# Two steps of VectorE's exponential chain placed on GpSimd, with a placing rule for the chain's products

## The chip, the cores and the metric

One core of one Trainium2 chip. The time is device time of one execution in microseconds (us). A run has a state: "slow" if it lies over 1.5% above the fastest run of the same kernel. The mean granted clock of TensorE is given with a run: 1.0 is full speed.

## The reference

```python
x = A_x                                   # 1 x 2048 x 640, bf16
xn = layernorm(x)
q, k, v = split_heads(xn @ wqkv)          # 32 heads of 20
s = softmax(q @ k.T * 20 ** -0.5) @ v @ wo
g = silu(mlp_over_tokens(layernorm(xn)))  # gelu inside, 2048 -> 1536 -> 2048
out = x + s * g
```

The softmax needs 32 x 2048 x 2048 exponentials. The kernel cuts them into 2048 units, each one PSUM bank of scores: 128 keys x 512 queries.

## The kernel before

A list scheduler in Python builds a fixed order of instructions for each engine, from a table of costs. At run time each engine follows its order and waits only on semaphores. TensorE (PE) writes scores into PSUM banks. ScalarE (ACT) takes two banks at a time through its exponential. VectorE (DVE) takes single banks (two of them, 4 and 5, each with its own buffers) through a chain of six instructions that builds the bits of an approximate exponential:

```python
ch = [
    (lambda e: e.tensor_scalar(w3, lo, 0x7FFF, None, ALU.bitwise_and), bs, [sw], dv(N)),            # mask, from PSUM
    (lambda e: e.tensor_scalar(v_, w_, 1.0 / 256.0, -128.0, ALU.mult, ALU.add), [sw], [sv], dv(N, .26)),   # linear
    (lambda e: e.tensor_scalar(l_, w_, a3 / 65536.0, (b3 - 64.0 * a3) / 256.0, ALU.mult, ALU.add),
     [sw], [sl_], dv(N, .26)),                                                                      # linear
    (lambda e: e.tensor_tensor(l_, v_, l_, ALU.mult), [sv, sl_], [sl_], dv(N, .52)),                # product
    (lambda e: e.tensor_tensor(l_, l_, w_, ALU.mult), [sl_, sw], [sl_], dv(N, .52)),                # product
    (lambda e: e.scalar_tensor_tensor(o_, zr, -(self.OFFS - 16256.0), l_, ALU.add, ALU.add),
     bs + [sl_], [S_(f"dpt{s0 + i}") for i in range(n)], dv(N)),                                    # last, from PSUM
]
# ... cut: the scheduler, each time an engine is free, takes the candidate that is ready first ...
if eng == "dve":
    for chn in dchains:
        (fn, rd, wr, cost) = chn[0][0]
        c.append((90.0 - 0.1 * len(chn), pr.ready("dve", rd, wr), lambda chn=chn: emit_dchain(chn)))
```

How many units go to DVE is not fixed: the scheduler gives it a new one whenever a DVE bank is free in its own clock. The rest stays with ACT.

The softmax here doesn't subtract the row's maximum and nothing guards it: scores larger than these inputs give would overflow.

Of the kernel before, what the change touches and what calls it, by code (L numbers as in the profile page):

```python
# [7 lines left out]
ALU = mybir.AluOpType  # L8
# [274 lines left out]
class _Kern:  # L283
# [25 lines left out]
    DVE_TAIL_GUARD = 3  # L309
    LAST_GUARD = 10  # L310
    NTMP = 4
    WARM = True
    WARM_MIN = 180.0
    WARM_SLACK = 30.0
# [87 lines left out]
    def schedule(self):  # L402
        pr, t = self.prog, self.t
# [21 lines left out]
        def S_(name):  # L425
            s = sl.get(name)
            if s is None:
                s = sl[name] = _Slot(name)
            return s
# [12 lines left out]
        def dv(n, rate=1.04):  # L442
            return 75.0 + n * rate
# [51 lines left out]
        def small(fn):  # L495
            def f(e):
# [12 lines left out]
                name="id1", cost=300)  # L509
# [5 lines left out]
               cost=200)  # L515
# [8 lines left out]
               writes=[S_("pad")], name="pad", cost=150)  # L524
        pr.dve(lambda e: e.tensor_reduce(cst_sb[:, 1:2], onerow, mybir.AxisListType.X, ALU.add), reads=[S_("idf")],
               writes=[S_("row")], name="pad", cost=130)
        for col, a_, b_, src in ((3, -1.0, 1.0, 0), (4, -CQ0, CQ0, 0), (5, QC, 0.0, 1), (6, KC, 0.0, 1)):
            pr.dve(lambda e, col=col, a_=a_, b_=b_, src=src: e.tensor_scalar(
                cst_sb[:, col:col + 1], cst_sb[:, src:src + 1], a_, b_, ALU.mult, ALU.add),
                reads=[S_("pad"), S_("row")], writes=[S_("cq")], name="cq", cost=90)  # L530
# [535 lines left out]
        dexp = []  # L1066
# [79 lines left out]
        def can_exp():  # L1146
            if not pexp:
                return False
            n = len(pexp[0][0])
            s0 = ptr[0] if ptr[0] + n <= self.RP else 0  # L1150
            return not any(pt_busy[s0:s0 + n])

        dchains = []

        def start_dchain():

            us, banks, grp = dexp[0]
            n = len(us)
            if dptr[0] + n > self.DPT:
                dptr[0] = 0  # L1160
            s0 = dptr[0]
            dexp.pop(0)
            for i in range(n):
                dpt_busy[s0 + i] = True
            dptr[0] = (s0 + n) % self.DPT
            N = n * 512
            zr = ps_all[:, banks[0] * 512:banks[0] * 512 + N]
            lo = zr.bitcast(u16).rearrange("p (n two) -> p n two", two=2)[:, :, 0:1]
            k = self.DVE_GROUPS.index(grp)
            w_, v_, l_ = ew_sb[:, k, 0:N], ev_sb[:, k, 0:N], el_sb[:, k, 0:N]  # L1170
            sw, sv, sl_ = S_(f"ew{k}"), S_(f"ev{k}"), S_(f"el{k}")
            w3 = w_.rearrange("p (n one) -> p n one", one=1)
            o_ = dpt_sb[:, s0:s0 + n, :].rearrange("p a b -> p (a b)").bitcast(u16)
            bs = [bank_slot[b] for b in banks[:n]]
            a3, b3 = self.C3
            ch = [
                (lambda e: e.tensor_scalar(w3, lo, 0x7FFF, None, ALU.bitwise_and), bs, [sw], dv(N)),  # L1177
                (lambda e: e.tensor_scalar(v_, w_, 1.0 / 256.0, -128.0, ALU.mult, ALU.add), [sw], [sv], dv(N, .26)),  # L1178
                (lambda e: e.tensor_scalar(l_, w_, a3 / 65536.0, (b3 - 64.0 * a3) / 256.0, ALU.mult, ALU.add),  # L1179
                 [sw], [sl_], dv(N, .26)),  # L1180
                (lambda e: e.tensor_tensor(l_, v_, l_, ALU.mult), [sv, sl_], [sl_], dv(N, .52)),  # L1181
                (lambda e: e.tensor_tensor(l_, l_, w_, ALU.mult), [sl_, sw], [sl_], dv(N, .52)),  # L1182
                (lambda e: e.scalar_tensor_tensor(o_, zr, -(self.OFFS - 16256.0), l_, ALU.add, ALU.add),  # L1183
                 bs + [sl_], [S_(f"dpt{s0 + i}") for i in range(n)], dv(N)),
            ]
            dchains.append([(x, us, s0, grp) for x in ch])

        def emit_dchain(chn):
            (fn, rd, wr, cost), us, s0, grp = chn.pop(0)
            tk = pr.dve(fn, reads=rd, writes=wr, name=f"dexp{us[0]}", cost=cost)  # L1190
            if not chn:
                dchains.remove(chn)
                dgrp_state[grp] = "free"
                for i, u in enumerate(us):
                    avail.append((tk.fin, u, "d", s0 + i))
# [320 lines left out]
        def pe_cands(T):  # L1516
# [29 lines left out]
            if avail and acc_ok[0]:  # L1546
# [14 lines left out]
                if pick:  # L1561
                    r = max(x[0] for x in pick) + PV_MARGIN
                    pr_ = 1.0 if nav >= self.PV_HI else 30.0 if ramp[0] else (8.0 if pr.gate.warm or not self.WARM else 70.0)
                    c.append((pr_, max(r, pr.ready("pe", [], [sl_acc])), lambda pick=pick: emit_pv(pick)))
            if self.WARM:
                wb = warm_bank()
# [18 lines left out]
            for j in active:  # L1585
                s = j.steps[j.i]
                if s[0] == "pe":
                    c.append((j.prio if pr.gate.warm or not self.WARM else -2.0, pr.ready("pe", s[2], s[3]),
                              lambda j=j: do_step(j, "pe")))
# [60 lines left out]
        def do_step(j, eng):  # L1650
            s = j.steps[j.i]
            j.i += 1
            if s[0] == "ev":
                n = s[8]
                fn = ev_fn(s, eng)
                cost = ac(n) if eng == "act" else dv(n, 0.55 if s[7].startswith("xTe") else 1.04)
                getattr(pr, eng)(fn, reads=s[5], writes=s[6], name=s[7], cost=cost)
            elif s[0] == "pe":
                pe_full(s[1], s[2], s[3], s[4], s[5])
            else:  # L1660
                getattr(pr, s[0])(s[1], reads=s[2], writes=s[3], name=s[4], cost=s[5])
            settle(j)

        def eng_cands(eng, T):
            c = []
            for j in active:
                s = j.steps[j.i]
                if s[0] == eng:
                    c.append((j.prio, pr.ready(eng, s[2], s[3]), lambda j=j: do_step(j, eng)))
                elif s[0] == "ev" and (eng == "dve" or (eng == "act" and (ramp[0]))):  # L1670
                    pen = 0.0 if eng == "dve" else 0.0
                    c.append((j.prio - 30.0 + pen, pr.ready(eng, s[5], s[6]), lambda j=j: do_step(j, eng)))
            if eng == "act" and can_exp():
                us, banks, grp = pexp[0]
                c.append((30.0 if ramp[0] else 48.0, pr.ready("act", [bank_slot[b] for b in banks[:len(us)]], []), emit_exp))
            if eng == "dve":
                for chn in dchains:
                    (fn, rd, wr, cost) = chn[0][0]
                    c.append((90.0 - 0.1 * len(chn), pr.ready("dve", rd, wr), lambda chn=chn: emit_dchain(chn)))
                if dexp and not any(ch[0][3] == dexp[0][2] for ch in dchains):  # L1680
                    us, banks, grp = dexp[0]
                    n = len(us)
                    s0 = dptr[0] if dptr[0] + n <= self.DPT else 0
                    if not any(dpt_busy[s0:s0 + n]):
                        r = pr.ready("dve", [bank_slot[b] for b in banks[:n]], [])

                        def go():
                            start_dchain()
                            emit_dchain(dchains[-1])
                        c.append((90.0, r, go))  # L1690
            return c

        def warm_bank():
            if nxt[0] < 12:
                return AB
            if WB in busybanks or WB in bank_off:
                return None
            return WB
# [18 lines left out]
        while True:  # L1717
# [26 lines left out]
            for e in order:  # L1744
                cs = pe_cands(pr.T[e]) if e == "pe" else eng_cands(e, pr.T[e])
                cs_by[e] = cs

            bt = None
            for e in order:
                if not cs_by[e]:  # L1750
                    continue
                r = min(max(x[1], pr.T[e]) for x in cs_by[e])
# [4 lines left out]
            r, e = bt  # L1757
            if e == "dve" and nxt[0] >= NU:

                soon = [max(x[1], pr.T[e]) for x in cs_by[e] if x[0] <= 12.0]  # L1760
                if soon and min(soon) <= r + 130.0:
                    r = min(soon)
# [45 lines left out]
```

## Time and profile before

| | us |
|---|---|
| time, median of 2 runs | 869.83 (867.17 to 872.49) |
| span of the profiled run | 864.8, clock 1.0 |
| busy: PE, DVE, ACT, GpSimd | 798.6, 823.5, 845.3, 14.0 |

Lines of the profile are read in the prediction; "idle before" is how long the engine stood still just ahead of these instructions, and what ended it.

### The profile page before, as it was taken

To read this page: it belongs to the slowest core of one execution; us is meant where nothing else is said; L and a number is where in the kernel's file an instruction comes from. 1 tells how busy PE (TensorE), PEld (TensorE's weight loads), DVE (VectorE), ACT (ScalarE), POOL (GpSimd) and SP (SyncE) were. 2 spreads that over 40 slices of the span, in tenths; PEclk is the share of its full clock that TensorE was granted. 3 is DMA by queue.
4 is the path that set the end of the run, shared out by engine and by line. 5 is a ranking of instruction groups with operands and counts; after the bars stand their busy time and mean duration, and the time that the engine had idled before them with its cause. 6 is when DMAs were issued, how large, how long until landed. Compare 5 with 4: busy or idle time off the path is not lost.

```text
span 864.8 us, 16498 instructions
## 1 busy us (share of the span) xinstructions
PE 798.6 (92%) x5828; PEld 257.1 (30%) x5918; DVE 823.5 (95%) x2047; ACT 845.3 (98%) x925; POOL 14.0 (2%) x23
## 2 busy tenths in 40 slices
PE   8899999999999999999999999999899998998997
PEld 5422222222222223222322222222222222232233
DVE  8889999999999999999999999999999999999996
ACT  7899999999999999999999999999999999999996
POOL 3200000000000000000000000000000000000000
PEclk9999999999999999999999999999999999999999
DMA  8241010011010313020013022123312201032121
GB/s 236 48 113 30 8 35 10 16 36 31 11 55 15 77 34 89 10 55 10 16 25 78 23 51 52 25 52 71 67 30 46 47 11 11 3 102 69 41 44 35
DMA packets 123350, 39.32 MB, mean 45 GB/s; under 512 B 84312, under 2 KB 122152, under 8 KB 123272
## 3 DMA queue, kind: packets, MB, share of 16 engines
q1 hardware_dynamic: 123272, 38.27, 19.3%
q8 instruction: 50, 0.82, 0.4%
q14 instruction: 28, 0.23, 0.1%
HBM read 25.88 MB, written 9.83 MB: 41 GB/s over the span
## 4 chain that ended last, share of the span: by engine, by line
ACT 87%; PE 10%; DVE 2%; issue 1%; ACTq 0%
ACT pt_sb L1137 85%; PE ps_all L1109 3%; PE ps_all L1224 1%; ACT zt_sb L843 1%; PE ps_all L755 1%; PE ps_all L1702 1%; PE ps_all L879 1%; ACT zt_sb L838 1%; DVE ew_sb L1177 0%; PE ps_all L683 0%; PE ps_all L1710 0%; PE ps_all L722 0%; PE ps_all L703 0%; DVE dpt_sb L1183 0%; DVE el_sb L1181 0%
## 5 line engine op out<-in xcount | busy, mean ns | idle before, releaser
L1137 ACT ACTIVATE pt_sb<-ps_all 128x1024 bf16<-128x1024 f32 x888 | 819.8, 1144 | 3.8 <-PE ps_all L1109 3.0
L1109 PE MATMUL ps_all<-qk_sb 32*128 32x512 bf16 (+1 forms) x2112 | 367.5, 377 | 48.7 <-ACT pt_sb L1137 37.0
L1177 DVE TENSOR_SCALAR ew_sb<-ps_all 128x512 uint16<-128x512 uint16 x272 | 184.2, 685 | 20.7 <-PE ps_all L1109 19.6
L1109 PEld LDWEIGHTS ps_all<-qk_sb 32*128 32x128 bf16 x2112 | 97.3, 91 | 347.2 <-ACT pt_sb L1137 300.7
L1183 DVE SCALAR_TENSOR_TENSOR dpt_sb<-ps_all,el_sb 128x512 uint16<-128x512 f32 x272 | 182.1, 684 | 1.8
L1224 PE MATMUL ps_all<-pt_sb,v_sb 128*32 128x512 bf16 (+1 forms) x1833 | 162.7, 378 | 0.3 <-issue 0.3
L1181 DVE TENSOR_TENSOR el_sb<-ev_sb,el_sb 128x512 bf16<-128x512 bf16 x272 | 111.1, 418 | 1.1
L1182 DVE TENSOR_TENSOR el_sb<-el_sb,ew_sb 128x512 bf16<-128x512 bf16 x272 | 110.3, 418 | 0.9
L1224 PE MATMUL ps_all<-dpt_sb,v_sb 128*32 128x512 bf16 (+1 forms) x279 | 83.7, 379 | 0.0
L810 PE MATMUL ps_all<-regB,regA 128*128 128x128 bf16 (+1 forms) x371 | 75.6, 300 | 2.9 <-issue 1.1
L1178 DVE TENSOR_SCALAR ev_sb<-ew_sb 128x512 bf16<-128x512 uint16 x272 | 75.3, 285 | 2.3
L810 PE MATMUL ps_all<-regC,regA 128*128 128x128 bf16 (+1 forms) x370 | 74.2, 300 | 1.8 <-issue 1.0
L1179 DVE TENSOR_SCALAR el_sb<-ew_sb 128x512 bf16<-128x512 uint16 x272 | 75.1, 284 | 0.0
L722 PE MATMUL ps_all<-xnT_sb,wqk_sb 128*112 128x512 bf16 x200 | 68.2, 405 | 0.4 <-DVE zt_sb L816 0.4
L1224 PEld LDWEIGHTS ps_all<-pt_sb,v_sb 128*32 128x32 bf16 x1833 | 35.4, 94 | 55.5 <-issue 50.4
L1702 PE MATMUL ps_all<-wrm_sb 128*128 128x512 bf16 (+1 forms) x117 | 35.2, 391 | 3.9 <-DVE ps_all L513 2.2
L810 PEld LDWEIGHTS ps_all<-regB,regA 128*128 128x128 bf16 x384 | 25.8, 97 | 39.1 <-issue 23.8
L810 PEld LDWEIGHTS ps_all<-regC,regA 128*128 128x128 bf16 x384 | 25.0, 97 | 39.8 <-issue 28.5
L1710 PE MATMUL ps_all<-wrm_sb,v_sb 128*128 128x512 bf16 x97 | 34.0, 385 | 1.3 <-issue 0.7
L755 PE MATMUL ps_all<-wv_sb,xnT_sb 128*128 128x160 bf16 (+1 forms) x160 | 33.8, 302 | 0.4 <-DVE pk_sb L1030 0.3
L879 PE MATMUL ps_all<-wo_sb,xnT_sb 128*128 128x128 bf16 (+3 forms) x152 | 30.4, 298 | 0.7 <-issue 0.5
L722 PEld LDWEIGHTS ps_all<-xnT_sb,wqk_sb 128*112 128x112 bf16 x200 | 20.7, 127 | 30.6 <-issue 13.4
(89 smaller groups left out, 354.9 us busy)
## 6 DMA issues: line engine op xcount, KB each, us to landing
regA<-in_B_w_dram SPq DMA_DIRECT2D x6, 1024.0 KB
regA<-in_B_w_dram SPq DMA_DIRECT2D x8, 768.0 KB
qkT_scratch_dram<-pk_sb SPq DMA_DIRECT2D x40, 112.0 KB
qk_sb<-qkT_scratch_dram SPq DMA_DIRECT2D x56, 80.0 KB
regA<-in_A_x_dram SPq DMA_DIRECT2D x6, 640.0 KB
on_scratch_dram<-on_sb SPq DMA_DIRECT2D x124, 20.0 KB
out_dram<-regC SPq DMA_DIRECT2D x3, 640.0 KB
wqk_sb<-in_A_wqkv_dram SPq DMA_DIRECT2D x2, 680.0 KB
```

Of the source, the lines that this page charges most:

```text
L722: steps.append(("pe", lambda e, dc=dc: e.matmul(ps_all[0:112, bk * 512:(bk + 1) * 512], wqk_sb[:, dc * 1280 + c0:dc * 1280 + c0 + 112], xn ...
L810: steps.append(("pe", lambda e, k=k: e.matmul(ps(bk, n), wap[:, k, col0:col0 + 128], rows[:, k, c0:c0 + n], start=(k == 0), stop=(k == nk ...
L1109: pr.pe(lambda e, outp=outp, lhsT=lhsT, rhs=rhs, g=g: e.matmul(outp, lhsT, rhs, start=True, stop=True, tile_position=(32 * g, 0)), reads=q ...
L1137: tk = pr.act(lambda e: e.activation(outp, inp, AF.Exp, bias=-self.OFFS * math.log(2.0) / 128.0, scale=math.log(2.0) / 128.0), reads=[bank ...
L1177: (lambda e: e.tensor_scalar(w3, lo, 0x7FFF, None, ALU.bitwise_and), bs, [sw], dv(N)),
L1178: (lambda e: e.tensor_scalar(v_, w_, 1.0 / 256.0, -128.0, ALU.mult, ALU.add), [sw], [sv], dv(N, .26)),
L1179: (lambda e: e.tensor_scalar(l_, w_, a3 / 65536.0, (b3 - 64.0 * a3) / 256.0, ALU.mult, ALU.add), [sw], [sl_], dv(N, .26)),
L1181: (lambda e: e.tensor_tensor(l_, v_, l_, ALU.mult), [sv, sl_], [sl_], dv(N, .52)),
L1182: (lambda e: e.tensor_tensor(l_, l_, w_, ALU.mult), [sl_, sw], [sl_], dv(N, .52)),
L1183: (lambda e: e.scalar_tensor_tensor(o_, zr, -(self.OFFS - 16256.0), l_, ALU.add, ALU.add), bs + [sl_], [S_(f"dpt{s0 + i}") for i in range( ...
L1224: pr.pe(lambda e, outp=outp, lhsT=lhsT, rhs=rhs, k=k, g=g: e.matmul(outp, lhsT, rhs, start=(k == 0), stop=(k == NB - 1), tile_position=(0, ...
L1702: pe_full(lambda e: e.matmul(ps(wb, n), wrm_sb[:, 0:P], wrm_sb[:, P:P + n], start=True, stop=True), [S_("warm"), S_("warm1")], [bank_slot[ ...
```

## The change

Intent: DVE is nearly full, GpSimd is empty. Put the two linear steps on GpSimd. I expected the products to collide with GpSimd's steps; that was not shown by the trace before, and the trace after shows it (beside a step they take 491 and 653 ns on the mean, elsewhere 419 and 417). So let DVE take a product (flag `port` in the code) only when the GpSimd steps placed so far are done, in the scheduler's clock. No semaphore enforces this: it only fixes positions in the order.

```diff
+    POOL_TS = 560.0
...
-    (lambda e: e.tensor_scalar(v_, w_, 1.0 / 256.0, -128.0, ALU.mult, ALU.add), [sw], [sv], dv(N, .26)),
+    (lambda e: e.tensor_scalar(v_, w_, 1.0 / 256.0, -128.0, ALU.mult, ALU.add), [sw], [sv], self.POOL_TS, "pool", True),
     (lambda e: e.tensor_scalar(l_, w_, a3 / 65536.0, (b3 - 64.0 * a3) / 256.0, ALU.mult, ALU.add),
-     [sw], [sl_], dv(N, .26)),
-    (lambda e: e.tensor_tensor(l_, v_, l_, ALU.mult), [sv, sl_], [sl_], dv(N, .52)),
-    (lambda e: e.tensor_tensor(l_, l_, w_, ALU.mult), [sl_, sw], [sl_], dv(N, .52)),
+     [sw], [sl_], self.POOL_TS, "pool", True),
+    (lambda e: e.tensor_tensor(l_, v_, l_, ALU.mult), [sv, sl_], [sl_], dv(N, .52), "dve", True),
+    (lambda e: e.tensor_tensor(l_, l_, w_, ALU.mult), [sl_, sw], [sl_], dv(N, .52), "dve", True),
...
+    if eng in ("dve", "pool"):
+        for chn in dchains:
+            (fn, rd, wr, cost, en, port) = chn[0][0]
+            if en == eng:
+                r = pr.ready(eng, rd, wr)
+                if eng == "dve" and port:
+                    r = max(r, pr.T["pool"])
+                c.append((90.0 - 0.1 * len(chn), r, lambda chn=chn: emit_dchain(chn)))
```

More of the change, by code (lines that the diff above doesn't have):

```diff
@@ L311 @@
     NTMP = 4
+    POOL_TT = 1150.0
+    POOL_TS = 560.0
     WARM = True
@@ L1176, in start_dchain @@
             ch = [
-                (lambda e: e.tensor_scalar(w3, lo, 0x7FFF, None, ALU.bitwise_and), bs, [sw], dv(N)),
-                (lambda e: e.tensor_scalar(v_, w_, 1.0 / 256.0, -128.0, ALU.mult, ALU.add), [sw], [sv], dv(N, .26)),
+                (lambda e: e.tensor_scalar(w3, lo, 0x7FFF, None, ALU.bitwise_and), bs, [sw], dv(N), "dve", False),
+                (lambda e: e.tensor_scalar(v_, w_, 1.0 / 256.0, -128.0, ALU.mult, ALU.add), [sw], [sv], self.POOL_TS, "pool", True),
                 (lambda e: e.tensor_scalar(l_, w_, a3 / 65536.0, (b3 - 64.0 * a3) / 256.0, ALU.mult, ALU.add),
-                 [sw], [sl_], dv(N, .26)),
-                (lambda e: e.tensor_tensor(l_, v_, l_, ALU.mult), [sv, sl_], [sl_], dv(N, .52)),
-                (lambda e: e.tensor_tensor(l_, l_, w_, ALU.mult), [sl_, sw], [sl_], dv(N, .52)),
+                 [sw], [sl_], self.POOL_TS, "pool", True),
+                (lambda e: e.tensor_tensor(l_, v_, l_, ALU.mult), [sv, sl_], [sl_], dv(N, .52), "dve", True),
+                (lambda e: e.tensor_tensor(l_, l_, w_, ALU.mult), [sl_, sw], [sl_], dv(N, .52), "dve", True),
                 (lambda e: e.scalar_tensor_tensor(o_, zr, -(self.OFFS - 16256.0), l_, ALU.add, ALU.add),
-                 bs + [sl_], [S_(f"dpt{s0 + i}") for i in range(n)], dv(N)),
+                 bs + [sl_], [S_(f"dpt{s0 + i}") for i in range(n)], dv(N), "dve", False),
             ]
@@ L1188, in emit_dchain @@
         def emit_dchain(chn):
-            (fn, rd, wr, cost), us, s0, grp = chn.pop(0)
-            tk = pr.dve(fn, reads=rd, writes=wr, name=f"dexp{us[0]}", cost=cost)
+            (fn, rd, wr, cost, eng, _), us, s0, grp = chn.pop(0)
+            tk = getattr(pr, eng)(fn, reads=rd, writes=wr, name=f"dexp{us[0]}", cost=cost)
             if not chn:
@@ L1675, in eng_cands @@
                 c.append((30.0 if ramp[0] else 48.0, pr.ready("act", [bank_slot[b] for b in banks[:len(us)]], []), emit_exp))
+            if eng in ("dve", "pool"):
[6 more added lines that the diff above has]
+                        c.append((90.0 - 0.1 * len(chn), r, lambda chn=chn: emit_dchain(chn)))
             if eng == "dve":
-                for chn in dchains:
-                    (fn, rd, wr, cost) = chn[0][0]
-                    c.append((90.0 - 0.1 * len(chn), pr.ready("dve", rd, wr), lambda chn=chn: emit_dchain(chn)))
                 if dexp and not any(ch[0][3] == dexp[0][2] for ch in dchains):
```

## The prediction

> **What bounds the kernel now.** I read the page's busy shares first, then the chain that ended last. The columns of the first line are busy time, share of the 864.8 us span and instruction count; the second is the chain's shares by engine.
>
> ```profile
> PE 798.6 (92%) x5828; PEld 257.1 (30%) x5918; DVE 823.5 (95%) x2047; ACT 845.3 (98%) x925; POOL 14.0 (2%) x23
> ...
> ACT 87%; PE 10%; DVE 2%; issue 1%; ACTq 0%
> ```
>
> ScalarE (ACT) is the bound: it is busy nearly all the time and carries 87% of the chain. VectorE (DVE) has next to nothing left either, and GpSimd (POOL) is empty. Next, the groups by line, columns: count, busy us, mean ns, idle us before and who ended it.
>
> ```profile
> L1137 ACT ACTIVATE pt_sb<-ps_all 128x1024 bf16<-128x1024 f32 x888 | 819.8, 1144 | 3.8 <-PE ps_all L1109 3.0
> ...
> L1177 DVE TENSOR_SCALAR ew_sb<-ps_all 128x512 uint16<-128x512 uint16 x272 | 184.2, 685 | 20.7 <-PE ps_all L1109 19.6
> L1183 DVE SCALAR_TENSOR_TENSOR dpt_sb<-ps_all,el_sb 128x512 uint16<-128x512 f32 x272 | 182.1, 684 | 1.8
> L1181 DVE TENSOR_TENSOR el_sb<-ev_sb,el_sb 128x512 bf16<-128x512 bf16 x272 | 111.1, 418 | 1.1
> L1182 DVE TENSOR_TENSOR el_sb<-el_sb,ew_sb 128x512 bf16<-128x512 bf16 x272 | 110.3, 418 | 0.9
> L1178 DVE TENSOR_SCALAR ev_sb<-ew_sb 128x512 bf16<-128x512 uint16 x272 | 75.3, 285 | 2.3
> L1179 DVE TENSOR_SCALAR el_sb<-ew_sb 128x512 bf16<-128x512 uint16 x272 | 75.1, 284 | 0.0
> ```
>
> The softmax exponentials are shared out in units of 512 columns: 888 ACT instructions of two units each, and 272 units on DVE by a chain of six instructions. 888 x 2 + 272 = 2048, all of them. So a unit that DVE does not take comes back to ACT at half an ACT instruction, and one ACT instruction takes 819.8 / 888 = 0.92 us (the mean of 1144 ns overlaps its neighbour).
>
> Durations on DVE overlap too, so I take the pitch (start to start) from the timeline of DVE; columns: start us, duration us.
>
> ```profile
> 398.68 0.29 DVE L1178 TENSOR_SCALAR ev_sb<-ew_sb 128x512 bf16<-128x512 uint16 x1
> 398.89 0.29 DVE L1179 TENSOR_SCALAR el_sb<-ew_sb 128x512 bf16<-128x512 uint16 x1
> 399.09 0.68 DVE L1177 TENSOR_SCALAR ew_sb<-ps_all 128x512 uint16<-128x512 uint16 x1
> 399.69 0.42 DVE L1181 TENSOR_TENSOR el_sb<-ev_sb,el_sb 128x512 bf16<-128x512 bf16 x1
> 400.02 0.29 DVE L1178 TENSOR_SCALAR ev_sb<-ew_sb 128x512 bf16<-128x512 uint16 x1
> ```
>
> A linear step (L1178, L1179) costs 0.20 us of DVE, a product (L1181, L1182) 0.33, the mask and the last step (L1177, L1183) 0.60 each: 2.27 us a chain, 617 us for 272. Last, who TensorE waits for when it writes new scores (total us, times, longest):
>
> ```profile
> PE ps_all L1109 <- ACT pt_sb L1137: 37.0, 117, 0.6
> ...
> PE ps_all L1109 <- DVE ew_sb L1177: 0.5, 1, 0.5
> ```
>
> It waits for ACT, as it should when ACT is the bound, and hardly ever for DVE. The kernel is emitted in a fixed order by a list scheduler with a table of costs; the page shows that the table fits DVE as it stands.
>
> [...] The two products have two SBUF inputs; the mask and the last step read PSUM and at most one SBUF tensor[...]. No overlap of the two engines exists in this trace[...]. [...] The trace has only small or writing instructions of GpSimd:
>
> ```profile
> 5.10 0.96 POOL L1301 MEMSET on_sb<- 128x1024 bf16 x1
> 5.99 0.63 POOL L1302 MEMSET wo_sb<- 128x640 bf16 x1
> ...
> 32.71 0.27 POOL L608 TENSOR_SCALAR st_sb<-st_sb 128x16 f32<-128x16 f32 x1
> ```
>
> From the two memsets the slope is (0.96 - 0.63) / 384 = 0.86 ns a column[...]. A 16-column TENSOR_SCALAR took 0.27 us; with that slope one of 512 is estimated at 0.27 + 496 x 0.00086 = 0.70 us in duration. The first memset's pitch is 0.89 where its duration is 0.96[...], so I estimate a pitch of 0.55 to 0.65. The kernel's new constant, 560 ns, is at the good end.
>
> **The change, part by part.** The order of both builds gives the counts.
> - Removed from DVE: 2 x 272 linear steps, 544 x 0.20 = 109 us.
> - The scheduler places 263 chains instead of 272: DVE loses another 9 x (2.27 - 0.40) = 17 us. In all 126 us of 823; DVE is no longer near a bound.
> - Added to GpSimd: 526 linear steps x 0.60 = 316 us. It has 850 us; hidden as throughput.
> - Added to ACT: 892 full and one half exponential instead of 888, +4.5 x 0.92 = **+4.2 us on the bound**. Nothing is taken from ACT. So even if all else stays hidden, the time is 869.8 + 4.2 = 874.
> - On TensorE the scores and products are the same in number; filler matmuls rise from 236 to 259, harmless.
> - Moved: each chain now crosses DVE, GpSimd, DVE. The linear steps' time in the chain goes from 0.40 us to two GpSimd steps and two semaphore crossings. The page of DVE waits has no such crossing now; the pitch of dependent GpSimd instructions at 32 us exceeds their duration by 0.08, so I take 0.1 each.
>
> What the last point costs decides. There are two score banks for DVE, and the built order mostly runs them as a pair: mask, mask, product, product, product, product, last, last. A bank is refilled when its chain ends. Before, the chains ran from 46 to 852 us, 806 us for 136 pairs: 5.9 us a pair, set by DVE's work. After, 131.5 pairs must fit in about 806 + 4 us: **6.16 us a pair** is allowed, because some 6.7 ACT exponentials lie between in TensorE's fixed order.
>
> What a pair takes, from these numbers: mask 0.60, crossing 0.1, four GpSimd steps one behind the other 4 x 0.56 = 2.24, crossing 0.1, product of the second chain 0.33, then the second product of both 0.66, last step of the first 0.60, then semaphore, scores into the bank and semaphore, about 1.0 (a 0.38 us matmul, TensorE's queue and the scheduler's 0.25 us grace). Sum 5.6 us. [...]the first chain's product becomes ready while GpSimd works for the second; in the scheduler's clock it waits for GpSimd[...], 0.33 to 0.4 us. Some 100 other DVE instructions with two SBUF inputs or dense bf16 SBUF copies (gelu, residual, normalisation) meet GpSimd half of the time: about 0.1 us a pair. Sum 6.0 to 6.1 us, against 6.16 allowed. With GpSimd at 0.62 instead of 0.56 it is 6.3, with 0.70 it is 6.6. Other DVE work queued in front (1.2 us a pair) only partly fits into the gaps.
>
> Each 0.1 us over costs up to 131 x 0.1 = 13 us, less what TensorE's 37 us of waiting for ACT absorbs (perhaps a third, since waits are spread otherwise). I choose 0.15 us over: about 20 us, less some absorbed, 15. So 869.8 + 4.2 + 15 = **889 us**.
>
> **The rivals.**
> 1. All hidden: GpSimd keeps to 0.56, the port rule works, ACT is fed. 872 to 878, "same". For it: the costs fitted well before, and DVE has 126 us of new slack. Against: the grace per pair is a tenth of a microsecond by my sum.
> 2. The chain through GpSimd becomes the bound: TensorE, in order, waits for a DVE bank, and ACT behind it starves. 890 to 950. For it: four serial GpSimd steps a pair, an order with no semaphore for the port rule (only the position is fixed, so the clash returns when the clocks drift), and conversion from uint16 that no row here prices. My centre lies at the mild end of this.
> 3. DVE relief makes it faster. Against it: ACT was the bound at 98% and gets more work. Only if ACT's idle 20 us fell could anything be won, and those lie at the start and the end (the first 40 us and the last 25), which the change doesn't touch. Below 1%.
>
> **Range and chances.** Rival 1 at a little over four in ten, rival 2 at a little under six: 889 us, 868 to 932. The same limit of 2% is 887, so faster 0.01, same 0.43, slower 0.56.
>
> **What would show it.** Right: ACT's exponential group x892 at an unchanged 0.92 us each, but with tens of us idle ended by TensorE's scores; TensorE's scores waiting for the DVE last step instead of only for ACT; DVE busy near 700 us; GpSimd near 300 us or more with pitch near 0.6 us; products of DVE with a longer mean than 418 ns where they meet GpSimd. Wrong on the good side: ACT idle unchanged and the scores still waiting only for ACT. Wrong on the bad side: GpSimd steps of 0.8 us or more, or durations on both engines that grow by each other's, with pairs at 7 us.

## The result, and the profile after

910.05 us (908.71 and 911.39) against 869.83: ratio 1.0462, 95% interval 1.031 to 1.0615. A ratio here compares the fast runs of both kernels in the same rounds, so it is not quite the ratio of the medians quoted. The change makes the kernel slower; the time lies in the predicted range, above the centre.

The page of the changed kernel: busy shares, the granted clock in 40 slices, and the chain that ended last.

```profile
PE 850.5 (94%) x5941; PEld 265.4 (29%) x5941; DVE 747.6 (82%) x1467; ACT 860.6 (95%) x930; POOL 375.9 (41%) x549
...
PEclk9999999999999999999999956999999999999999
...
DVE 31%; PE 25%; ACT 19%; POOL 19%; issue 5%; DMA 1%; DVEq 0%; ACTq 0%; SPq 0%; POOLq 0%
```

Before, 87% of the chain was ACT. Now it wanders through DVE, PE, GpSimd and ACT: the loop of a DVE bank (scores, mask, GpSimd, products, last step, scores) is on the path. And two of the 40 slices have a clock of 0.5 and 0.6, which before had none. The costliest groups (columns as in the prediction):

```profile
L1139 ACT ACTIVATE pt_sb<-ps_all 128x1024 bf16<-128x1024 f32 x893 | 833.1, 1062 | 29.8 <-PE ps_all L1111 26.8
...
L1180 POOL TENSOR_SCALAR ev_sb<-ew_sb 128x512 bf16<-128x512 uint16 x263 | 187.0, 711 | 475.6 <-DVE ew_sb L1179 467.5
...
L1183 DVE TENSOR_TENSOR el_sb<-ev_sb,el_sb 128x512 bf16<-128x512 bf16 x263 | 116.7, 448 | 85.8 <-POOL el_sb L1181 85.6
L1181 POOL TENSOR_SCALAR el_sb<-ew_sb 128x512 bf16<-128x512 uint16 x263 | 174.8, 665 | 16.5
...
L1184 DVE TENSOR_TENSOR el_sb<-el_sb,ew_sb 128x512 bf16<-128x512 bf16 x263 | 122.6, 482 | 2.7
```

ACT now stands idle 29.8 us ahead of its exponentials instead of 3.8, for scores that are late. The products take 448 and 482 ns on the mean instead of 418. GpSimd's steps take 711 and 665 ns; the minimum and the median of both are 617 and 618, so the rest of the mean is stretching. The waits, by engine and line (total us, times, longest; PEld is TensorE loading the weights of the same matmul):

```profile
PEld ps_all L1111 <- DVE dpt_sb L1185: 35.0, 78, 1.6
...
PE ps_all L1111 <- ACT pt_sb L1139: 19.7, 70, 0.9
...
PE ps_all L1111 <- DVE dpt_sb L1185: 11.5, 29, 1.3
```

TensorE now waits for the last step of the DVE chain to free a bank, and less for ACT: on PE 19.7 us instead of 37.0, on its weight loads 247.0 instead of 300.7. Its order is fixed, so ACT's next scores stand behind that wait.

Two timelines show the collision (start us, duration us). First GpSimd:

```profile
406.89 0.62 POOL L1180 TENSOR_SCALAR ev_sb<-ew_sb 128x512 bf16<-128x512 uint16 x1 [2.44 <-DVE ew_sb L1179]
407.57 0.62 POOL L1181 TENSOR_SCALAR el_sb<-ew_sb 128x512 bf16<-128x512 uint16 x1
408.26 0.86 POOL L1180 TENSOR_SCALAR ev_sb<-ew_sb 128x512 bf16<-128x512 uint16 x1
409.18 0.69 POOL L1181 TENSOR_SCALAR el_sb<-ew_sb 128x512 bf16<-128x512 uint16 x1
```

Then DVE in the same stretch:

```profile
408.22 0.43 DVE L1183 TENSOR_TENSOR el_sb<-ev_sb,el_sb 128x512 bf16<-128x512 bf16 x1 [0.35 <-POOL el_sb L1181]
408.68 0.71 DVE L1184 TENSOR_TENSOR el_sb<-el_sb,ew_sb 128x512 bf16<-128x512 bf16 x1
409.43 0.69 DVE L1185 SCALAR_TENSOR_TENSOR dpt_sb<-ps_all,el_sb 128x512 uint16<-128x512 f32 x1
```

Undisturbed, GpSimd's pitch is 0.68 to 0.69 us (406.89, 407.57, 408.26), not the 0.56 that the scheduler believes. At 408.22 the first product of one chain starts as GpSimd begins the other chain's step: GpSimd's 0.62 becomes 0.86, and the second product's 0.42 becomes 0.71. The rule does not exclude this. The scheduler's own times were read: both products of this very chain already lie beside a GpSimd step, for 0.17 and 0.34 us. Of the 526 products, 101 lie beside a step in the scheduler's times, and 179 do in the trace; the other 78 arise where the chip's times differ from the scheduler's.

Counted over the whole trace, a first product beside a GpSimd step takes 491 ns on the mean, a second one 653; elsewhere they take 419 and 417. GpSimd's steps take 786 ns where they meet a product and 634 elsewhere. The mask and the last step, which read PSUM, stay at 684 ns, as before, and beside a step they take 682 and 686.

The slow clock: around 513 us one GpSimd step takes three times its length. Its line in the timeline:

```profile
512.41 1.87 POOL L1181 TENSOR_SCALAR el_sb<-ew_sb 128x512 bf16<-128x512 uint16 x1
```

Beside it, in the timeline of DVE, lies a gelu instruction that the rule doesn't cover:

```profile
512.98 0.81 DVE L850 TENSOR_TENSOR regC<-zt_sb 128x1280 bf16<-128x1280 bf16 x1
```

The stretches of 3.4 us that follow, with their length, TensorE's busy time (instructions), clock, DMA share and GB/s:

```profile
513.30:516.70 3.40, 3.05 (x19) 1.00 0.85 235
516.70:520.10 3.40, 2.21 (x15) 0.80 0.00 0
520.10:523.50 3.40, 3.40 (x11) 0.50 0.00 0
```

TensorE waits up to 1.6 us for that chain's bank, and the clock halves, for 41 us in all. The second stretch straddles the drop, as its mean clock of 0.80 shows; in the trace's record of the clock the drop is at 518.71, and in the 3.4 us before it TensorE was busy for 1.86. While the clock is half, TensorE is busy without a gap (40.95 us of 40.95) and ACT waits for it: it runs 27 exponentials in these 41 us, where the kernel before runs 45 in the same stretch. At 0.92 us each, an estimate of what this spell costs is some 16 us. I had not predicted this.

### The profile page after: what moved, and what is told of

Same layout as the page of the kernel before. It is cut to its first block, busy times and chain, and to the rows that moved or that the text cites.

```text
span 907.1 us, 16643 instructions
## 1 busy us (share of the span) xinstructions
PE 850.5 (94%) x5941; PEld 265.4 (29%) x5941; DVE 747.6 (82%) x1467; ACT 860.6 (95%) x930; POOL 375.9 (41%) x549
## 4 chain that ended last, share of the span: by engine, by line
DVE 31%; PE 25%; ACT 19%; POOL 19%; issue 5%; DMA 1%; DVEq 0%; ACTq 0%; SPq 0%; POOLq 0%
ACT pt_sb L1139 18%; PE ps_all L1111 10%; POOL ev_sb L1180 9%; POOL el_sb L1181 8%; DVE dpt_sb L1185 8%; DVE ew_sb L1179 6%; PE ps_all L1226 5%; DVE el_sb L1184 5%; DVE el_sb L1183 5%; PE ps_all L812 4%; PE ps_all L724 1%; PE ps_all L881 1%; DVE zt_sb L818 1%; PE ps_all L1709 1%; DVE tr_sb L1276 1%
## 5 line engine op out<-in xcount | busy, mean ns | idle before, releaser
L1139 ACT ACTIVATE pt_sb<-ps_all 128x1024 bf16<-128x1024 f32 x893 | 833.1, 1062 | 29.8 <-PE ps_all L1111 26.8
L1111 PE MATMUL ps_all<-qk_sb 32*128 32x512 bf16 (+1 forms) x2112 | 383.5, 384 | 37.5 <-ACT pt_sb L1139 19.7
L1180 POOL TENSOR_SCALAR ev_sb<-ew_sb 128x512 bf16<-128x512 uint16 x263 | 187.0, 711 | 475.6 <-DVE ew_sb L1179 467.5
L1111 PEld LDWEIGHTS ps_all<-qk_sb 32*128 32x128 bf16 x2112 | 99.5, 91 | 355.3 <-ACT pt_sb L1139 247.0
L1179 DVE TENSOR_SCALAR ew_sb<-ps_all 128x512 uint16<-128x512 uint16 x263 | 175.1, 684 | 28.2 <-PE ps_all L1111 27.2
L1181 POOL TENSOR_SCALAR el_sb<-ew_sb 128x512 bf16<-128x512 uint16 x263 | 174.8, 665 | 16.5
L1185 DVE SCALAR_TENSOR_TENSOR dpt_sb<-ps_all,el_sb 128x512 uint16<-128x512 f32 x263 | 175.5, 684 | 2.2
L1184 DVE TENSOR_TENSOR el_sb<-el_sb,ew_sb 128x512 bf16<-128x512 bf16 x263 | 122.6, 482 | 2.7
L812 PE MATMUL ps_all<-regB,regA 128*128 128x512 bf16 (+1 forms) x384 | 84.7, 319 | 1.3 <-DVE pk_sb L1032 0.9
L1717 PE MATMUL ps_all<-wrm_sb,v_sb 128*128 128x512 bf16 x150 | 52.8, 389 | 0.4 <-DVE tr_sb L1276 0.2
L881 PE MATMUL ps_all<-wo_sb,xnT_sb 128*128 128x512 bf16 (+3 forms) x160 | 32.3, 303 | 0.7 <-DVE regC L895 0.5
```

The lines of the kernel that those rows point to most:

```text
L812: steps.append(("pe", lambda e, k=k: e.matmul(ps(bk, n), wap[:, k, col0:col0 + 128], rows[:, k, c0:c0 + n], start=(k == 0), stop=(k == nk ...
L1111: pr.pe(lambda e, outp=outp, lhsT=lhsT, rhs=rhs, g=g: e.matmul(outp, lhsT, rhs, start=True, stop=True, tile_position=(32 * g, 0)), reads=q ...
L1139: tk = pr.act(lambda e: e.activation(outp, inp, AF.Exp, bias=-self.OFFS * math.log(2.0) / 128.0, scale=math.log(2.0) / 128.0), reads=[bank ...
L1717: pe_full(lambda e: e.matmul(ps(AB), zero, wrm_sb[:, P:P + 512], start=new, stop=new), [S_("warm"), S_("v_ones")], [sl_acc], "warmz", 512)
```

## The experiments

Theories at the start. A: the GpSimd step is under-priced (0.685 us, not 0.56), and with four of them in a row per pair of chains TensorE's order asks for banks too early. B: blocking, that is, products and GpSimd steps that take longer where they meet (491 and 653 ns instead of 419 and 417, 786 instead of 634), which no constant prices. C, suggested by the trace: stalls of TensorE (busy for 1.86 us of 3.4) bring its clock down (to 0.5 for 41 us), which costs on its own. Each kernel was run four times, beside seven runs of the kernel before on the same chip (medians 866.92, 867.31 and 867.01 for e1 to e4, e5 to e8, e9 to e11).

### e1: the scheduler told the true pitch

```diff
-    POOL_TS = 560.0
+    POOL_TS = 685.0
```

> One constant of the changed kernel: the scheduler is told 685 ns a GpSimd step (the pitch that the trace of the changed kernel shows) instead of 560. The built order then has 247 chains and 900.5 exponentials on ScalarE, 12.5 more than before, 12.5 x 0.92 = 11.5 us. Theory A (the step was under-priced, so TensorE's order asks for a bank that is not yet free): the waits for the last step of the chain nearly vanish, no slow-clock spell, 880 to 888 us. Theory B[...]: it stays above 898 us.

883.66 us, ratio 1.0213 (1.0169 to 1.0256). In the range of A. The group of exponentials in its trace:

```profile
L1139 ACT ACTIVATE pt_sb<-ps_all 128x1024 bf16<-128x1024 f32 (+1 forms) x901 | 832.2, 1118 | 5.5 <-PE ps_all L1111 4.3
```

ACT's idle time falls from 29.8 to 5.5 us, though the products still take 453 and 463 ns and GpSimd's steps 679 and 692. TensorE's waits for the chain's last step fall from 35.0 and 11.5 us (weight loads and matmuls) to 8.4 and 0.2. Blocking is still there, if in fewer places (148 of 494 products lie beside a step); an order with more room for it hardly stalls. The room is paid for with 16 fewer chains and 8 more exponentials on ACT. One of its runs had a clock of 0.986 and took 891.4.

### e2: GpSimd steps that only write

```diff
-    e.tensor_scalar(v_, w_, 1.0 / 256.0, -128.0, ALU.mult, ALU.add)   # and the other linear step
+    e.memset(jk_sb[:, 2 * k, :], 0.0)                                 # 744 columns of scratch
```

ev and el are zeroed once at the start. The order on the other engines is that of the changed kernel, instruction for instruction. Its output is wrong, which doesn't matter for the time.

> The order of the changed kernel to the instruction on TensorE, VectorE and ScalarE, but each GpSimd step is a memset of 744 columns of scratch: about the same length (0.69 us estimated), no SBUF read. The result is wrong on purpose. Theory B (blocking by GpSimd's reads): products back at 418 ns, GpSimd steps no longer stretched, and 870 to 885 us. Theory A (length of the GpSimd steps, one behind the other): products back at 418 ns, but 895 us or more.

875.08 us, ratio 1.0094 (1.0077 to 1.0111).

```profile
L1185 POOL MEMSET jk_sb<- 128x744 bf16 x263 | 190.0, 722 | 0.0
...
L1187 DVE TENSOR_TENSOR el_sb<-ev_sb,el_sb 128x512 bf16<-128x512 bf16 x263 | 110.0, 421 | 73.1 <-POOL jk_sb L1185 71.4
L1188 DVE TENSOR_TENSOR el_sb<-el_sb,ew_sb 128x512 bf16<-128x512 bf16 x263 | 105.8, 419 | 2.7
```

The products are back at 421 and 419 ns. The memsets are as long as wanted: pitch 0.66 us in the timeline, and four in a row take 3 x 0.66 + 0.72 = 2.70 us against 3 x 0.685 + 0.62 = 2.67. So A's length is all there, and the excess is gone. As many products as in the changed kernel, 180, lie beside a GpSimd step, and they take 420 and 422 ns. Length alone is not the cause: B, as expected.

### e3 and e6: shorter steps, still reading

```diff
-    e.tensor_scalar(v_, w_, ...)                        # 512 columns, both linear steps
+    e.tensor_scalar(v_[:, 0:368], w_[:, 0:368], ...)    # e3; 0:440 in e6
```

Again the same order on the other engines, and slightly wrong.

> The order of the changed kernel to the instruction, but each GpSimd step works on 368 of 512 columns, so that its pitch is about 0.56 us as the scheduler thinks (0.685 less 144 x 0.00086). The result is slightly wrong on purpose. Theory A: 874 to 884 us, no slow-clock spell. Theory B: the steps still read SBUF and still collide, 893 us or more.

> The order of the changed kernel, GpSimd steps on 440 of 512 columns: halfway between e3 (368, 874 us) and the changed kernel (512, 910 us), pitch 0.62 us. Wrong on purpose. If the excess is a threshold (slack of a pair used up first, stalls and a slow-clock spell after it): 875 to 882 us, clock 0.999. If it grows in proportion to the step from 368 columns on: 890 to 894.

e3: 874.16 us, ratio 1.0084 (1.0069 to 1.0099), as A expected. e6: 879.48, ratio 1.0128 (1.0094 to 1.0161), clock 0.996 to 0.997.

```profile
L1183 POOL TENSOR_SCALAR ev_sb<-ew_sb 128x368 bf16<-128x368 uint16 x263 | 150.3, 572 | 505.8 <-DVE ew_sb L1182 498.3
...
L1187 DVE TENSOR_TENSOR el_sb<-el_sb,ew_sb 128x512 bf16<-128x512 bf16 x263 | 115.3, 455 | 2.7
```

In e3 the steps are 0.50 us long at a pitch of 0.56 where undisturbed, but 572 ns on the mean, and the second product takes 455: they collide and it costs nothing. So blocking alone is not the cause either. From 368 to 440 columns the time rises by 5 us, from 440 to 512 by 24 to 31, or by some 14 without slow-clock spells (893 us, estimated under e10). So the rise is not in proportion, which asked for 890 to 894 at 440 columns, but more than half of the bend is the clock's. e6's clock was not the 0.999 that I expected: its profiled run has a spell of 6.8 us, at 828, behind a wait for a DMA. The reading that fits e2, e3 and e6 is that the order has some slack per pair; the longer steps use it up, and blocking then falls on the path. Either one alone fits.

### e4: without the rule

```diff
-    if eng == "dve" and port:
+    if False and port:
```

> The changed kernel without its second part: products may be placed while GpSimd works. The built order has 281 chains and 883.5 exponentials on ScalarE, 4.1 us less than before. If the rule earns its keep: products and GpSimd steps much longer than now, more waits, 920 us or more. If it does nothing on the chip (only positions are fixed): 900 to 915. If the rule only costs chains: below 900.

Two runs at 937.01 and 938.28 (clock 0.963, 0.961), two at 976.4 that count as slow (0.90). Fast runs: ratio 1.0816 (1.0795 to 1.0838). The scheduler packs 281 chains and takes 4.5 exponentials off ACT against before, and the kernel is slower than with the rule. The time is as expected; what I expected to see with it is not. In the profiled run, which is a slow one, GpSimd's steps take 720 and 655 ns and the products 429 and 497, hardly longer than with the rule, and 212 of 562 products lie beside a step, against 179 of 526. ACT stands idle 91.2 us for scores. So the rule is worth its place, but not shown to be so by keeping the engines apart; it also makes the scheduler pack fewer chains, and this run doesn't separate the two.

### e5: more filler matmuls for the clock

```diff
-    WARM_OVER = 3600.0        # columns of filler matmuls wanted per stretch; WARM_ACC, WARM_FLOOR alike
+    WARM_OVER = 4200.0
```

> The changed kernel with the scheduler's four limits for filler matmuls raised from 3600 or 4200 columns to 4200: the built order has 385 fillers instead of 286 (all shapes), 264 chains and 892 exponentials. If the slow-clock spell of 41 us (in e1's own four runs some 23 us of slow clock went with 8 us) is a consequence of stalls leaving TensorE short of work, it disappears and takes 12 to 16 us with it: 894 to 900 us with clock 0.999. If the spell is only a companion and costs nothing of its own: 906 to 913. If the fillers get in ScalarE's way: above 913.

899.06 us, ratio 1.0369 (1.0319 to 1.0418); clock 1.0 in two runs, 0.998 and 0.989 in the others. In the profiled run the 41 us spell is gone, and the products (439, 512 ns) and ACT's idle (20.4 us) stay bad. That is 11 us less than the changed kernel in its first two runs, a little under the 12 to 16 expected, but only 3 to 5 less than in e10, where its spells were shorter. With more work for TensorE the clock was 0.989 to 1.0 in these four runs, against 0.961 to 0.987 in e10's (the run at 0.989, 905.87 us, still had spells), which fits that they follow from its lack of work. The order is not quite the same (264 chains) and e5 and e10 ran on different chips, so this is no exact difference.

### e10: the changed kernel again

> The changed kernel unedited, on the chip and in the rounds of the others: 907 to 912 us with a mean clock of 0.975, as before, if the slow-clock spell belongs to the kernel; about 895 with clock 0.999 in some runs if the spell is chance.

901.55, 903.23 and 903.94 us (clock 0.987, 0.984, 0.983), and 919.76 (0.961, slow). Ratio 1.0414 (1.0396 to 1.0431). The clock was below 0.99 in every run, so spells belong to the kernel, but their length varies: 20.5 us in the profiled run, at the same place in the order (518.6 us), 41 before. My expectation of 907 or more was missed for that reason. Over the five fast runs of this kernel, 0.987 to 0.975 in clock goes with 901.55 to 911.39 us, about 0.8 us for each 0.001. Taken on to 0.998, near e2 and e3 and outside the clocks that were measured, this gives an estimate of 893 us without spells. The first profiled run agrees: 908.71 less the 16 us estimated for its spell.

### e9: products that read PSUM

```diff
-    e.tensor_tensor(l_, v_, l_, ALU.mult)
+    e.tensor_scalar(l_[:, 0:256], zr[:, 0:256], 0.0, None, ALU.mult)     # zr is PSUM
```

and the second product alike on columns 256 to 511. Same order. Its output is wrong, which doesn't matter for the time.

> The order of the changed kernel to the instruction, but the two products of each chain read 256 columns of PSUM instead of two SBUF tensors: about the same length (0.34 us pitch estimated)[...]. GpSimd's steps are untouched; only the gelu, residual and normalisation instructions of VectorE can still collide with them. Wrong on purpose. If the chain's own products are the collisions that count: 872 to 882 us, GpSimd steps near 618 ns on the mean. If the long other instructions are (the trace shows one GpSimd step of 1.87 us beside one of them, just ahead of the slow-clock spell): 895 us or more.

877.09, 880.07 and 886.2 us at clocks 0.998, 0.993, 0.985, and 890.73 (0.978, slow). Ratio 1.0162 (1.0114 to 1.021). In part outside what I expected (872 to 882), because of spells, which stayed. The profiled run is the slow one; it has a spell of 37.5 us at the same place in the order, behind a stretch of 3.4 us in which TensorE was busy 2.19, and just ahead of it the same GpSimd step took 1.87 us beside the same gelu instruction, as it did in e10 (1.87 at 512.87, with the gelu instruction's 0.81 at 513.46). So the collision with the gelu instruction was left in, and the spell with it. GpSimd's steps:

```profile
L1181 POOL TENSOR_SCALAR el_sb<-ew_sb 128x512 bf16<-128x512 uint16 x263 | 167.6, 637 | 16.5
L1180 POOL TENSOR_SCALAR ev_sb<-ew_sb 128x512 bf16<-128x512 uint16 x263 | 166.6, 634 | 484.7 <-DVE ew_sb L1179 476.4
```

637 and 634 ns instead of 665 and 711. As in e2, 180 products lie beside a step, and they take 418 and 421 ns. At clock 0.998 it takes 877 us (one run) against the 893 estimated for the changed kernel: leaving spells aside, the chain's own products are the collisions that count, about 16 us. The gelu and residual instructions leave about 2 us against e2, and the spells.

### e11: the rule for the gelu, residual and normalisation instructions too

```diff
+    if eng == "dve" and s[4].rstrip("0123456789_") in ("sq", "p", "t", "g", "res", "epm"):
+        r = max(r, pr.T["pool"])
```

> The changed kernel with its placing rule extended to VectorE's other instructions[...] (gelu, residual, normalisation of the attention output). The built order has 261 chains and 893.5 exponentials, +0.9 us on ScalarE. If the long instructions are the collisions that count: 876 to 890 us. If the chain's own products are, or if the rule cannot hold on the chip because the steps are under-priced: 900 us or more.

894.33, 899.33, 905.5 (clock 0.999, 0.992, 0.981) and 914.42 (0.965, slow); ratio 1.0377 (1.0319 to 1.0434). No better than e10 beyond the noise of the spells, which agrees with e9. All runs lie above the first range that I gave, and two of the three fast ones below the second (900 or more). In the trace of the changed kernel these instructions, too, take longer beside a GpSimd step: gelu's products 959 ns on the mean and 814 elsewhere, its linear steps 788 and 480, the residual 795 and 481, the normalisation 660 and 482. This rule, too, is one-sided: in the scheduler's times 28 of these 93 instructions still lie beside a GpSimd step, against 42 without it. Its run at 0.999 also supports the estimate of 893.

### e7 and e8: meant to beat both

Only the first linear step on GpSimd, no placing rule. e8 with 685 ns for a GpSimd step; e7 with 720 ns, 60 ns more for the linear step and 30 for each product on DVE.

```diff
-    [sw], [sl_], self.POOL_TS, "pool", True),     # second linear step
+    [sw], [sl_], dv(N, .26) + 60.0, "dve", True), # e7; e8 without the 60
```

> A version meant to beat both: only the first linear step on GpSimd, the second back on VectorE, no rule about placing, and the blocking priced into the scheduler (720 ns a GpSimd step, 60 more for the linear step and 30 more for each product on VectorE). The built order has 277 chains and 885.5 exponentials, 2.5 fewer than before, 2.3 us. If the price covers the blocking: 863 to 867 us. If blocking comes in clumps that a mean price does not cover: 872 or more.

> As e7 without the price for blocking (685 ns a step, VectorE's costs as before): 286 chains and 881.5 exponentials, 6.5 fewer than before, 6.0 us. If one GpSimd step a chain leaves slack enough: 860 to 866. If blocking eats it as in the kernel with both steps and no rule (937 us): 890 or more, with slow-clock spells.

e7: 876.8 us, ratio 1.0095 (1.0061 to 1.0128). e8: 887.8 to 891.34 in the fast runs, ratio 1.023 (1.0178 to 1.0282). Both missed their aim: e7 came out in its other branch (872 or more), e8 at the edge of its own (890 or more). The linear step left on DVE took 463 ns (e7) and 444 (e8) instead of 284, while the products stayed at 413 and 414: it is now what collides. None of the versions tried beats the kernel before.

## Why the prediction was right or wrong, point by point

- **ACT is the bound and gets 4.5 more exponentials, +4.2 us**: the count came out (893 instructions, one of them half). e2 and e3, which hardly stall, are 7 to 8 us above before, so some 3 to 4 us beyond this term were not in my sum. In e3 ACT is busy 6.3 us longer than before where the term is 4.2: the cost of one exponential was not quite unchanged, as I had it.
- **Length of a GpSimd step**: duration estimated 0.70, measured 0.618; pitch estimated 0.55 to 0.65 and used at 0.56, measured 0.685. I had taken it that a step's pitch is shorter than its duration, as for a memset (0.89 against 0.96 us in the trace before); it is longer. This term was mis-sized: 4 x 0.125 = 0.5 us a pair.
- **Blocking, 0.33 to 0.4 us a pair and 0.1 for other instructions**: my estimate, since the trace before has no product beside a GpSimd step; right in size. The stretching of GpSimd is 93 + 47 ns a chain and that of the products 30 + 64, which is 2 x 0.234 = 0.47 us a pair if all of it counts.
- **A pair against the 6.16 us allowed**: the allowance was right, since e2 and e3 run at 6.18 and 6.17 us a pair from the first mask to the last step. With the measured pitch my sum gives 6.5 to 6.6, 0.4 us over; by my own rule that is 131 x 0.4 = 52 us, some 35 after a third is absorbed. The chip shows an excess of 22. So the sum or its conversion into time was too large, and this covered in part for the pitch that was too small.
- **"No overlap of the two engines exists in this trace"**: misread. In the first 38 us there are some (GpSimd's 0.27 us step at 32.71 beside a VectorE instruction of 0.44 us at 32.42), but none with a tensor_tensor of VectorE, so that trace doesn't show what a product and a GpSimd step do to each other.
- **Which wait appears**: right. Scores wait for DVE's last step (0.2 us before, 11.5 after on PE; 5.3 before, 35.0 after on its weight loads), ACT's idle time is ended by scores, the products lengthen, DVE falls, though to 748 rather than near 700, GpSimd is at 376. Of DVE's 50 us too many, the stretched products are 263 x 0.094 = 25.
- **Excess over the 4.2**: 15 us predicted. Without spells the chip gives an estimate of 893 - 867 - 4 = 22.
- **The clock**: not in the prediction. Slow-clock spells added 8 to 18 us to those 893, run by run. This is most of the distance between 889 and 910, or 903 in the second set.
- **Rivals**: the second was right, and the mechanism with it. That 889 lies only 4 us from the estimate without spells is partly luck: it was chosen between two rivals, with a pitch too small and a conversion too large. The first (all hidden) is what e3 shows the kernel would do with the step at the length that the scheduler assumed: 874.

Open: why the GpSimd step at 512.41 took 1.87 us where its own 0.62 and the gelu instruction's 0.81 make 1.43; why spells last 20.48 us (e10), 37.55 (e9) or 40.96 (the changed kernel) with TensorE shown busy for most of it, when e6's ends after 6.8 and e8's three drops share some 14 us (estimated from its clock of 0.992 over 889.2 us); what exactly starts one, since the least busy stretch comes just before the drop in the changed kernel (1.86 of 3.4 us) and in e6 (1.72), but in e8 drops follow 2.55, 2.55 and 2.41 and none follows stretches of 2.48 and 2.49; and the exact share of length and blocking, which don't simply add up.

## What to carry to other kernels

Work moved to an empty engine is free in throughput only; where it lengthens a loop that returns a buffer, compare the loop with the period that the order allows before and after. A fixed order is as good as its cost table: measure the new instruction alone and next to what runs beside it (here a GpSimd step took 634 ns on the mean, and 786 beside a product), before the scheduler packs anything against it. When small stalls come up on an in-order TensorE, look at the granted clock next: here it cost 8 to 18 us, next to 22 for the stalls. And a placing rule that only one of two engines obeys doesn't keep them apart: read the scheduler's own times before you trust it.

## What a step costs, as measured

- Two-input products collided with a GpSimd step that reads (beside one they took 491 and 653 ns instead of 419 and 417), and not with one that only writes (e2: 420 and 422). The worst case was a GpSimd step of 1.87 us, against 0.62 + 0.81.
- From 368 columns (e3) to 512 the length of a GpSimd step rises by (0.618 - 0.498) / 144 = 0.83 ns a column. The same bf16 step has a pitch of 0.685 us on GpSimd and 0.20 on VectorE. The part of a GpSimd step that doesn't depend on its columns is estimated from these two lengths at 0.2 us. Its pitch is 0.067 us longer than its duration, where that of e2's memset is 0.06 us shorter (0.66 against 0.72).
- The granted clock fell to 0.5 behind 3.4 us with TensorE busy for 1.86, and stayed there for 40.96 us with TensorE busy in the trace.
